# A transducer joint with its backward pass: the label rows are spread over the partitions by transfers and a VectorE shuffle, and the last chunk puts two labels on 128 partitions

## The chip, the cores and the metric

One core of one Trainium2 chip. The time is the device time of one execution in microseconds (us), the median of 3 runs for the kernel before. TensorE is PE, VectorE is DVE, ScalarE is ACT, GpSimd is POOL; SP only issues transfers.

## The reference

Inputs are bf16: `x` [2, 16000, 256], two 3-tap convolution weights `w1`, `w2`, the label rows `g` [2, 8, 256], and three 256x256 matrices. The kernel returns the output and the gradients of all seven inputs (`vjp` with `grad_out`, [2, 4000, 8, 256]).

```python
h  = gelu(conv3(x, w1))[:, ::2]           # 8000 steps
f  = gelu(conv3(h, w2))[:, ::2]           # 4000 steps
fe = f @ w_f                              # b t e
ge = g @ w_g                              # b u e, 8 rows for each b
j  = tanh(fe[:, :, None, :] + ge[:, None, :, :])
out = j @ w_o                             # b t u v
```

For each step t and each label u the forward pass needs a tanh of `fe + ge` and a 256x256 product. The gradient of `w_o` contracts `j` with `grad_out` over all t and u, with t on the partitions; the gradient with respect to `j` multiplies `grad_out` by the transpose of `w_o`.

## The kernel before

The 2 x 4000 steps are one line of 8000, cut into 17 chunks (lines 257 to 261): the first has 256 steps, 15 have 512, and the last has 64, a half block of 128. Chunk 8 holds steps of both batches, and its first 40 partitions belong to batch 0 (`c.px`, line 280). In each round of the loop at line 1069 three stages are put down for neighbouring chunks: `stage_j` for chunk k, `stage_a` (both convolutions and `fe`) for chunk k+1, `stage_de` (everything backward of `fe`) for chunk k-1.

Nothing is issued in the order of the program text. `Flow.op` records every operation with an engine (or a choice of ACT and DVE), a cost, its dependencies and a priority, the time `F.now` or `at` in units of steps. `Flow.issue` (lines 107 to 205) then simulates the engines with these costs and always takes the operation that can start first; the priority decides between operations that can start at the same time. So an operation of low priority is put wherever its engine would otherwise stand idle in the simulation. `lag` adds time to the moment from which an operation counts as ready. Each engine then runs its own operations in exactly the order found. Buffers come from classes with a fixed number of slots ("jt" 3, "gx" 3, "out" 3, "geb" 2, "ps" 7 banks of PSUM), given out in the order of the program text except for "ps".

What the change touches:

- `make_geb` (line 602) makes `GEB`, the 8 rows of `ge` of one batch on all 128 partitions. It does this by matmuls whose stationary operand is one column of `gT` repeated 128 times: 16 matmuls of 256 columns and four evacuations of 128x512 (`evac`, line 341, on ACT or DVE) for each of three versions: batch 0, batch 1, and "x", the mixture for chunk 8. The last needs `GM`, a stationary operand built by two POOL copies in an "out" buffer. `make_ge` (line 1034) makes `gT` and, separately, `GE`, the same rows with the label features on partitions.
- `stage_j`, `pair(up)`: for the labels 2up and 2up+1, ACT makes `JT` = tanh(`FE` + `GE`) with features on partitions (line 644). The gradient of `w_o` needs j with steps on partitions, `JR`. In chunks 0 and 1 (`TRANS`) PE transposes `JT` and an evacuation copies it (line 663). From chunk 2 on DVE adds `FER` and `GEB` (line 668) and ACT takes the tanh (line 673); this is the only reader of `GEB`. `FER` is `FE` transposed by PE (line 593, `rows`). Then follow the `GWO` matmuls (line 681), the products with `WOT` (line 694), a chain on DVE that sums their gradients into `NGFE` (lines 716 to 731), the output products (line 744) with evacuation into `OUT`, and one store.
- The last chunk has 64 steps and thus uses 64 of the 128 partitions in `JR`, `GO`, `OUT` and in their matmuls. `load_go` and `load_got` load `grad_out` for all eight labels at once there.
- In `stage_de`, `put` (line 940) stores the gradient of `x` from SP's queue.

```python
257    sizes = [2 * P]
258    while NP - sum(sizes) > CW:
259        sizes.append(CW)
260    sizes.append(NP - sum(sizes))
264    TRANS = (0, 1)
```

Of the kernel before, what the change touches and what calls it, by code (L numbers as in the profile page):

```python
# [12 lines left out]
ALU = mybir.AluOpType  # L13
# [207 lines left out]
def kernel(  # L221
# [99 lines left out]
    W2T = fixed([P, KT, KK * D], BF16, "W2T")  # L321
    W1T = fixed([P, KT, KK * D], BF16, "W1T")
    GR8 = fixed([U, B, D], BF16, "GR8")
    ACC1 = fixed([P, KK, KT, D], FP32, "ACC1")
# [95 lines left out]
    def load_go(k, up, at, after=()):  # L420
        c = chunks[k]
        A, Pw = c.A, c.Pw
        GO = buf("go", [P, NB, 2, V], BF16, "GO")
        if c.last:

            dma("SP", lambda: GO[:Pw].rearrange("p a u v -> p (a u v)"),
                lambda: bass.AP(tensor=go_.tensor, offset=go_.offset + c.c0 * U * V, ap=[[U * V, Pw], [1, U * V]]),
                r=[], w=[GO], bytes_=Pw * U * V * 2, new=[GO], at=at, after=after)
# [109 lines left out]
    def stage_a(k, t0, dt):  # L538
# [45 lines left out]
        for mt in range(KT):  # L584
# [13 lines left out]

    n_gwo = sum(len(c.blk) for c in chunks) * U * KT
    gwo_cnt = [0]  # L600

    def make_geb(kind):
        GEB = buf("gx" if kind == "x" else "geb", [P, U, D], BF16, "GEB")
        if kind == "x":
            px = [c.px for c in chunks if c.px is not None][0]
            GM = buf("out", [P, KT, U, P], BF16, "GM")
            for b, lo, hi in ((0, 0, px), (1, px, P)):
                op("POOL", 1200.0, lambda e, b=b, lo=lo, hi=hi: nc.gpsimd.tensor_copy(
                    out=GM[:, :, :, lo:hi], in_=gT[b][:].unsqueeze(3).to_broadcast([P, KT, U, hi - lo])),
                   r=[gT[b]], w=[(GM, b)], new=[GM] if b == 0 else [])  # L610
            rd = [GM]
        else:
            rd = [gT[kind]]
        for u2 in range(UP):
            ps = psum()

            def mms(e, u2=u2, ps=ps):
                for j in range(2):
                    u = 2 * u2 + j
                    for kt in range(KT):  # L620
                        lhsT = GM[:, kt, u, :] if kind == "x" else gT[kind][:, kt, u:u + 1].to_broadcast([P, P])
                        mm(ps[:, j * D:(j + 1) * D], lhsT, WG[:, kt, :], kt == 0, kt == KT - 1)
            op("PE", c_pe([D] * 4), mms, r=rd + [WG], w=[ps], new=[ps] + ([GEB] if u2 == 0 else []))
            evac(lambda u2=u2: GEB[:, 2 * u2:2 * u2 + 2].rearrange("p u d -> p (u d)"), lambda ps=ps: ps[:], 512,
                 r=[ps], w=[(GEB, u2)])
        return GEB

    def stage_j(k, t0, dt, GEB):
# [3 lines left out]
        FE = S["FE"]  # L632

        def pair(up):
# [4 lines left out]
            u0 = up if c.last else 0  # L639
            for j in range(2):  # L640
                for mt in range(KT):
                    def jt(e, j=j, mt=mt):
                        for b, lo, hi, _ in c.segs:
                            nc.scalar.activation(  # L644
                                out=fl(JT[:, j, mt, :W], A)[:, :, lo:hi], in_=FE[:, 0:A, mt, lo:hi], func=ACT.Tanh,
                                bias=GE[:, b, mt, 2 * up + j:2 * up + j + 1], scale=1.0)
                    op("ACT", sum(c_act((s[2] - s[1]) * A, ptr=True) for s in c.segs), jt,
                       r=[(FE, mt)] + [(GE, s[0]) for s in c.segs], w=[(JT, (j, mt))],
                       new=[JT] if j == 0 and mt == 0 else [], at=tu - q * (1.0 - (2 * j + mt) / 4), sub="jt")
            halves = [c.blk[h:h + 2] for h in range(0, A, 2)]  # L650
            for h, tbs in enumerate(halves):
                JR = buf("jr", [P, 2, 2, D], BF16, "JR")
                th = tu + q * (h / 2 - 0.5)
                n, lo, m = len(tbs), tbs[0][0], Pw
                if k in TRANS:
                    tr = psum(BF16)
# [19 lines left out]
                def gwo(e, tbs=tbs, JR=JR):  # L676
                    for tb, m in tbs:
                        for j in range(2):
# [6 lines left out]
            OUT = buf("out", [P, NB, 2, V], BF16, "OUT_SB")  # L685
            for step in range(4):
# [5 lines left out]
                def gj(e, j=j, d2=d2, ps=ps):  # L692
                    for kt in range(KT):
                        mm(fl(ps[:, :W], A), WOT[:, kt, d2 * P:(d2 + 1) * P], GOT[:, u0:u0 + A, j, kt, :Pw], kt == 0, kt == KT - 1)
                if u and d2 == 0:
                    NGZ = buf("ngz", [P, KT, CW], FP32, "NGZ")
                op("PE", c_pe([W] * KT), gj, r=[GOT, WOT], w=[ps], new=[ps, NGZ] if u and d2 == 0 else [ps])
                if d2 == 0:
                    JSQ = buf("jsq", [P, KT, CW], BF16, "JSQ")

                    def jsq(e, j=j, JSQ=JSQ):
                        if e == "ACT":
                            nc.scalar.activation(out=JSQ[:, :, :W], in_=JT[:, j, :, :W], func=ACT.Square)  # L703
                        else:
                            nc.vector.tensor_tensor(out=JSQ[:, :, :W], in0=JT[:, j, :, :W], in1=JT[:, j, :, :W], op=ALU.mult)
                    op(("ACT", "DVE"), (c_act(KT * W), c_dve(KT * W, 0.5)), jsq, r=[(JT, (j, 0)), (JT, (j, 1))], w=[JSQ],
                       new=[JSQ], at=F.now - q / 4, sub="jsq")
# [68 lines left out]
    def stage_de(k, t0, dt):  # L776
# [136 lines left out]
        for bl, m in c.sblk:  # L913
# [21 lines left out]
            if bl % 2 == 1 or bl == A - 1:  # L935
# [130 lines left out]
    make_ge()  # L1066
    GEB = make_geb(0)
    GEBX = None
    for k in range(NG + 1):
# [15 lines left out]
        if k + 1 < NG and chunks[k + 1].px is not None:  # L1085
            F.now = t0 + Wk * 0.3
            GEBX = make_geb("x")
        if k < NG:
            F.stage = "j" + part(k)
            stage_j(k, t0, Wk, GEBX if c.px is not None else GEB)  # L1090
        if k < NG and c.px is not None:
            F.now = t0 + Wk * 0.3
            GEB = make_geb(1)
        if k + 1 < NG:
# [42 lines left out]
```

## Time and profile before

| | before |
|---|---|
| median of 3 runs | 795.49 us (794.16 to 795.92) |
| the profiled execution | 793.3 us, span 791.0 us, granted PE clock 0.998 |
| busy: PE, DVE, ACT, POOL | 98%, 91%, 92%, 11% |
| HBM traffic | 51.42 MB read, 50.34 MB written |

The span runs from the first to the last record; 2.3 us of the profiled time lie around it. Busy time of PE is modelled: a matmul of 256 columns is shown with 273 ns, while in a row of such matmuls one starts every 109 ns, so a pause of less than the difference leaves no trace in the busy share. Rows of a chain or a timeline therefore show better than a share how fast PE works. "L336" is the line of the helper that issues nearly all matmuls, so groups are told apart by their tiles. "Idle before" is what an engine waited for just before an instruction, not what slowed the kernel.

### The profile page before, as it was taken

What the parts mean: (1) busy time and instruction counts of PE and PEld (TensorE: products, weight loads), DVE (VectorE), ACT (ScalarE), POOL (GpSimd) and SP (SyncE); (2) the same over time, 40 slices, a digit from 0 to 9 for tenths busy, and PEclk for the clock granted to TensorE, in tenths of its full rate; (3) what the DMA queues carried; (4) which work ended last, traced back from release to release, by engine and by line L of the source; (5) the groups of instructions that cost most, each with busy time, mean ns of one, the idle gap of its engine ahead of it and who ended that gap; (6) DMA issues with size and microseconds to landing.
All of it is one profiled execution on the core that took longest, in us unless ns stands there. A gap on an engine that the chain in (4) does not pass through costs nothing.

```text
span 791.0 us, 15682 instructions
## 1 busy us (share of the span) xinstructions
PE 773.1 (98%) x5687; PEld 537.9 (68%) x5722; DVE 716.1 (91%) x1514; ACT 727.0 (92%) x1176; POOL 83.8 (11%) x227
## 2 busy tenths in 40 slices
PE   8989999999999999999999999999999999999996
PEld 6657577576675767767677675776767767577764
DVE  5899999897998989999999898989989899899874
ACT  6999999999999998999999998999999999898752
POOL 2110010201002011110101102010020110102010
PEclk9999999999999999999999999999999999999999
DMA  9999999999999899999999999998999999999874
GB/s 208 205 190 202 214 263 229 244 228 281 202 231 256 231 238 195 229 267 219 233 218 254 228 217 233 214 264 209 230 235 214 239 237 228 237 264 255 201 177 123
DMA packets 381809, 178.82 MB, mean 226 GB/s; under 512 B 307586, under 2 KB 375460, under 8 KB 379812
## 3 DMA queue, kind: packets, MB, share of 16 engines
q1 hardware_dynamic: 380516, 177.03, 99.8%
q8 instruction: 45, 0.74, 0.4%
q10 hardware_dynamic: 1056, 0.52, 0.2%
q14 instruction: 32, 0.26, 0.1%
q0 software_dynamic: 160, 0.27, 0.1%
HBM read 51.42 MB, written 50.34 MB: 129 GB/s over the span
## 4 chain that ended last, share of the span: by engine, by line
PE 72%; ACT 11%; DVE 9%; DMA 3%; issue 3%; SPq 1%; POOL 0%; DVEq 0%; ACTq 0%
PE ps L336 60%; PE GWO L336 10%; ACT JT L644 2%; DVE g_s L516 2%; ACT JSQ L703 2%; DMA GOT<-GO 2%; ACT g_sq L510 2%; PE psb L489 2%; DVE NGZ L716 1%; ACT OUT_SB L345 1%; ACT JR L673 1%; DVE g_sq L529 1%; SPq L360 1%; ACT HTo L513 1%; DMA XC<-in_x_dram 1%
## 5 line engine op out<-in xcount | busy, mean ns | idle before, releaser
L644 ACT ACTIVATE JT<-FE,GE 128x512 bf16<-128x512 bf16 (+4 forms) x288 | 180.7, 680 | 0.0
L716 DVE SCALAR_TENSOR_TENSOR NGZ<-JSQ,ps 128x512 f32<-128x512 bf16 (+3 forms) x252 | 149.7, 607 | 2.5 <-PE ps L336 2.0
L336 PE MATMUL ps<-WO,JT 128*128 128x256 bf16 (+1 forms) x1008 | 148.2, 273 | 1.3 <-DVE NGZ L716 1.3
L336 PE MATMUL ps<-GOT,WOT 128*128 128x512 bf16 (+2 forms) x544 | 146.5, 362 | 1.8 <-DMA GOT<-GO 1.6
L345 ACT CAST OUT_SB<-ps 128x512 bf16<-128x512 f32 (+1 forms) x210 | 123.0, 600 | 17.4 <-PE ps L336 17.3
L703 ACT ACTIVATE JSQ<-JT 128x1024 bf16<-128x1024 bf16 (+2 forms) x128 | 128.6, 1005 | 9.2 <-DVE NGZ L716 8.2
L336 PEld LDWEIGHTS <-JT 128*128 128x128 bf16 (+1 forms) x1008 | 98.2, 98 | 54.9 <-issue 2.0
L336 PE MATMUL GWO<-GO,JR 128*128 128x256 bf16 (+1 forms) x1008 | 130.8, 273 | 0.1
L673 ACT ACTIVATE JR<-JR 128x1024 bf16<-128x1024 bf16 (+1 forms) x116 | 121.6, 1054 | 4.1 <-DVE JR L668 3.8
L733 DVE TENSOR_TENSOR ZS<-ZS,NGZ 128x1024 f32<-128x1024 f32 (+2 forms) x102 | 115.1, 1128 | 0.3
L336 PEld LDWEIGHTS <-JR 128*128 128x128 bf16 (+1 forms) x1008 | 98.2, 98 | 17.8 <-issue 1.3
L516 DVE SCALAR_TENSOR_TENSOR g_s<-g_sq,ps 128x512 bf16<-128x512 bf16 (+2 forms) x102 | 65.2, 639 | 41.0 <-ACT HTo L513 32.2
L336 PEld LDWEIGHTS <-W 128*128 128x128 bf16 x612 | 58.1, 98 | 59.5 <-issue 2.2
L336 PE MATMUL ps<-XC,W 128*128 128x512 bf16 (+2 forms) x408 | 84.3, 362 | 0.9 <-DMA XC<-in_x_dram 0.9
L668 DVE TENSOR_TENSOR JR<-FER,GEB 128x1024 bf16<-128x1024 bf16 (+1 forms) x116 | 79.2, 684 | 2.2 <-PE GWO L336 1.0
L336 PEld LDWEIGHTS <-X 128*128 128x128 bf16 (+1 forms) x756 | 73.8, 98 | 9.4
L772 DVE TENSOR_TENSOR ACC<-ACC,ps 128x512 f32<-128x512 f32 x90 | 59.4, 678 | 16.9 <-PE ps L336 16.7
L336 PEld LDWEIGHTS <-WOT 128*128 128x128 bf16 x544 | 51.6, 98 | 23.9 <-DMA GOT<-GO 1.8
L347 ACT ACTIVATE GX_SB<-ps 128x512 bf16<-128x512 f32 (+1 forms) x109 | 64.1, 615 | 1.6 <-PE ps L336 1.1
L510 ACT ACTIVATE g_sq<-ps 128x512 bf16<-128x512 f32 (+2 forms) x102 | 59.1, 580 | 3.4 <-PE ps L336 2.7
L525 ACT ACTIVATE g_s<-g_s 128x1024 bf16<-128x1024 bf16 (+2 forms) x51 | 52.1, 1025 | 6.3 <-DVE g_s L516 6.1
L336 PE MATMUL ps<-GHoR,X 128*128 128x256 bf16 (+1 forms) x378 | 57.7, 273 | 0.0
(139 smaller groups left out, 1113.6 us busy)
## 6 DMA issues: line engine op xcount, KB each, us to landing
GO<-in_grad_out_dram SPq DMA_DIRECT2D x60, 512.0 KB, 5.3
out_dram<-OUT_SB SPq DMA_DIRECT2D x60, 512.0 KB, 5.3
X<-in_x_dram SPq DMA_DIRECT2D x15, 1088.0 KB, 8.3
out_dram<-GX_SB SPq DMA_DIRECT2D x30, 512.0 KB, 5.5
GO<-in_grad_out_dram SPq DMA_DIRECT2D x5, 256.0 KB, 5.4
GOT<-GO SPq DMA_TRANSPOSE x65, 5.0
out_dram<-OUT_SB SPq DMA_DIRECT2D x4, 256.0 KB, 3.5
XC<-in_x_dram SPq DMA_TRANSPOSE x62, 5.5
```

Source lines behind the costliest of these rows:

```text
L336: nc.tensor.matmul(ps_ap, lhsT=lhsT, rhs=rhs, start=start, stop=stop)
L345: nc.scalar.copy(out=dst(), in_=src())
L347: nc.scalar.activation(out=dst(), in_=src(), func=ACT.Copy, scale=scale)
L510: op("ACT", c_act(W, True), lambda e, mt=mt, ps=ps: nc.scalar.activation(out=sq[:, 0:A, mt, :Pw], in_=fl(ps[:, :W], A), func=ACT.Square, s ...
L516: op("DVE", c_dve(W), lambda e, mt=mt, ps=ps: nc.vector.scalar_tensor_tensor(out=s[:, 0:A, mt, :Pw], in0=sq[:, 0:A, mt, :Pw], scalar=1.0, ...
L644: nc.scalar.activation(out=fl(JT[:, j, mt, :W], A)[:, :, lo:hi], in_=FE[:, 0:A, mt, lo:hi], func=ACT.Tanh, bias=GE[:, b, mt, 2 * up + j:2 ...
L668: op("DVE", c_dve(n * 2 * D, 0.5), lambda e, lo=lo, n=n, m=m, JR=JR: nc.vector.tensor_tensor(out=JR[:m, 0:n], in0=S["FER"][:m, lo:lo + n]. ...
L673: op("ACT", c_act(n * 2 * D), lambda e, n=n, m=m, JR=JR: nc.scalar.activation(out=JR[:m, 0:n], in_=JR[:m, 0:n], func=ACT.Tanh), r=[JR], w= ...
L703: nc.scalar.activation(out=JSQ[:, :, :W], in_=JT[:, j, :, :W], func=ACT.Square)
L716: nc.vector.scalar_tensor_tensor(out=fl(zap(), A)[:, :, lo:hi], in0=fl(JSQ[:, d2, :W], A)[:, :, lo:hi], scalar=1.0, in1=fl(ps[:, :W], A)[: ...
L733: nc.vector.tensor_tensor(out=a, in0=a, in1=b, op=ALU.add)
L772: op("DVE", c_dve(512), lambda e: nc.vector.tensor_tensor(out=acc_ap().rearrange("p k d -> p (k d)"), in0=acc_ap().rearrange("p k d -> p ( ...
```

## The change

`make_geb` no longer uses matmuls. `ge_rows` computes the 8 rows once for each batch with two matmuls and one evacuation of 8x256 into `GER`. `make_geb` clears `GEB` on POOL, copies the eight rows (4 KB) by four transfers of POOL's queue to partitions 0, 32, 64 and 96, and one `stream_shuffle` on DVE copies the first partition of each group of 32 to the other 31, with the data seen as fp32. The shuffle's `lag` is 45000 ns for batch 0 and 100000 ns for batch 1. `mix_geb` makes the mixture for chunk 8 by two DVE copies. `ge_rows` and batch 0 are put down in round k = 1, batch 1 and the mixture ahead of chunk 8.

In the last chunk the two labels of a pair lie side by side: 64 steps of one on partitions 0 to 63, of the other on 64 to 127. `GO` is loaded by two transfers, `GOT` by one transpose of 128 x 1024, `JR` comes from two PE transposes of `JT` with an evacuation of 128x256 instead of the add and the tanh (and `FER` isn't made), `GWO` and the output take two matmuls for each pair instead of four, and the output is stored by two transfers after the fourth pair instead of by one after each. The gradient of `x` for the last chunk is stored from ACT's queue.

```diff
+            for j in range(2):
+                dma("SP", lambda j=j: GO[j * Pw:(j + 1) * Pw].rearrange("p a u v -> p (a u v)")[:, 0:UP * V].rearrange(
+                        "p (a v) -> p a v", v=V),
+                    lambda j=j: bass.AP(tensor=go_.tensor, offset=go_.offset + (c.c0 * U + j) * V,
+                                        ap=[[U * V, Pw], [2 * V, UP], [1, V]]),
+                    r=[], w=[(GO, j)], bytes_=Pw * UP * V * 2, new=[GO] if j == 0 else [], at=at, after=after)
...
-            dma("SP", lambda: GOT[:, :, :, :, :Pw].rearrange("p a u k c -> p (a u k) c"),
-                lambda: GO[:Pw].rearrange("p a u v -> p (a u v)"), r=[GO], w=[GOT],
+            dma("SP", lambda: GOT[:].rearrange("p a u k c -> p (a u k) c")[:, 0:UP * KT, 0:2 * Pw],
+                lambda: GO[:2 * Pw].rearrange("p a u v -> p (a u v)")[:, 0:UP * V], r=[GO], w=[GOT],
                 bytes_=Pw * U * V * 2, new=[GOT], transpose=True, at=at)
             st[k]["GOT"] = {up: GOT for up in range(UP)}
             return
...
-        if k not in TRANS:
+        if k not in TRANS and not c.last:
             S["FER"] = rows(k, "fer", "FER", FE, 0, A, [(FE, 0), (FE, 1)], pe=Pw, lag=0.0 if c.first else 500.0)
...
-    def make_geb(kind):
-        GEB = buf("gx" if kind == "x" else "geb", [P, U, D], BF16, "GEB")
-        if kind == "x":
-            px = [c.px for c in chunks if c.px is not None][0]
-            GM = buf("out", [P, KT, U, P], BF16, "GM")
-            for b, lo, hi in ((0, 0, px), (1, px, P)):
-                op("POOL", 1200.0, lambda e, b=b, lo=lo, hi=hi: nc.gpsimd.tensor_copy(
-                    out=GM[:, :, :, lo:hi], in_=gT[b][:].unsqueeze(3).to_broadcast([P, KT, U, hi - lo])),
-                   r=[gT[b]], w=[(GM, b)], new=[GM] if b == 0 else [])
-            rd = [GM]
-        else:
-            rd = [gT[kind]]
-        for u2 in range(UP):
+    def make_geb(b):
+
+        GEB = buf("geb", [P, U, D], BF16, "GEB")
+        op("POOL", 2100.0, lambda e: nc.gpsimd.memset(GEB[:], 0.0), r=[(GER, b)], w=[GEB], new=[GEB])
+        for q in range(0, P, 32):
+            dma("POOL", lambda q=q: GEB[q:q + 1], lambda: GER[:, b, :], r=[(GER, b)], w=[(GEB, q)], bytes_=4096)
+
+        def spread(e):
+            v = GEB[:].rearrange("p u d -> p (u d)").bitcast(FP32)
+            nc.vector.stream_shuffle(v, v, [0] * 32)
+        op("DVE", 66.0 + c_dve(U * D // 2), spread, r=[GEB], w=[GEB], sub="geb", lag=45000.0 if b == 0 else 100000.0)
+        return GEB
+
+    def mix_geb(G0, G1):
+        px = [c.px for c in chunks if c.px is not None][0]
+        GEB = buf("gx", [P, U, D], BF16, "GEB")
+        op("DVE", c_dve(U * D, 0.25), lambda e: nc.vector.tensor_copy(out=GEB[:], in_=G1[:]), r=[G1], w=[GEB], new=[GEB])
+        op("DVE", c_dve(U * D, 0.25), lambda e: nc.vector.tensor_copy(out=GEB[:px], in_=G0[:px]), r=[G0], w=[GEB])
+        return GEB
...
+    def ge_rows():
+        for b in range(B):
...
+            def mms(e, b=b, ps=ps):
+                for kt in range(KT):
+                    mm(ps[:U, 0:D], gT[b][:, kt, :], WG[:, kt, :], kt == 0, kt == KT - 1)
+            op("PE", c_pe([D] * KT), mms, r=[gT[b], WG], w=[ps], new=[ps])
+            evac(lambda b=b: GER[:, b], lambda ps=ps: ps[:U, 0:D], D, r=[ps], w=[(GER, b)])
...
+                if c.last:
+                    tr = psum(BF16)
+
+                    def trs(e, tr=tr):
+                        for kt in range(KT):
+                            nc.tensor.transpose(out=tr[:2 * Pw, kt * P:(kt + 1) * P], in_=JT[:, 0, kt, :2 * Pw], identity=ident[:])
+                    op("PE", c_pe([P] * KT), trs, r=[JT, ident], w=[tr], new=[tr], at=th, sub="jr")
+                    evac(lambda JR=JR: JR[:2 * Pw, 0, 0], lambda tr=tr: tr[:2 * Pw, 0:D], D, r=[tr], w=[JR], new=[JR], f=0.58)
+                elif k in TRANS:
...
-                        for j in range(2):
+                        for j in range(1 if c.last else 2):
                             for d2 in range(KT):
                                 n = gwo_cnt[0]
-                                mm(GWO[:, d2, :], JR[:m, tb % 2, j, d2 * P:(d2 + 1) * P], GO[:m, up if c.last else tb, j, :],
+                                rhs = (GO[:2 * m].rearrange("p a u v -> p (a u v)")[:, up * V:(up + 1) * V] if c.last
+                                       else GO[:m, tb, j, :])
+                                mm(GWO[:, d2, :], JR[:2 * m if c.last else m, tb % 2, j, d2 * P:(d2 + 1) * P], rhs,
                                    n == 0, n == n_gwo - 1)
                                 gwo_cnt[0] = n + 1
-                op("PE", c_pe([V] * (4 * n)), gwo, r=[JR, GO], w=[], at=tu + q * (h / 2 + 0.3), sub="gwo")
...
+                    if c.last:
+                        def out_last(e, m=m, ps=ps):
+                            for kt in range(KT):
+                                mm(ps[:2 * m, 0:V], JT[:, 0, kt, :2 * m], WO[:, kt, :], kt == 0, kt == KT - 1)
+                        op("PE", c_pe([V] * 2), out_last, r=[JT, WO], w=[ps], new=[ps] + ([OUT] if up == 0 else []), sub="out")
+                        evac(lambda m=m: OUT[:2 * m, up, 0], lambda m=m, ps=ps: ps[:2 * m, 0:V], V, r=[ps], w=[(OUT, up)])
+                        continue
...
+            if c.last:
+                for j in range(2 if up == UP - 1 else 0):
+                    dma("SP", lambda j=j: bass.AP(tensor=o_.tensor, offset=o_.offset + (c.c0 * U + j) * V,
+                                                  ap=[[U * V, Pw], [2 * V, UP], [1, V]]),
+                        lambda j=j: OUT[j * Pw:(j + 1) * Pw, 0:UP, 0], r=[OUT], w=[], bytes_=Pw * UP * V * 2)
+                return
...
-                    dma("SP", lambda: row_ap(gx_, row + 4 * A * p0 + lo, 4 * A, p1 - p0, hi - lo),
+                    dma("ACT" if c.last else "SP", lambda: row_ap(gx_, row + 4 * A * p0 + lo, 4 * A, p1 - p0, hi - lo),
...
             F.now = t0 + Wk * 0.3
-            GEBX = make_geb("x")
+            GEB1 = make_geb(1)
+            GEBX = mix_geb(GEB, GEB1)
+        if k == 1:
+            F.now = t0 + Wk * 0.1
+            ge_rows()
+            GEB = make_geb(0)
```

Left out: the lines that name the two-label layout in the same way in the other operations of the last chunk, and the counts that follow from it.

More of the change, by code (lines that the diff above doesn't have):

```diff
@@ L597, in stage_a @@
         S["FR"] = rows(k, "fr", "FR", FT, 0, A, None, pe=Pw)
-    n_gwo = sum(len(c.blk) for c in chunks) * U * KT
+    n_gwo = sum(len(c.blk) * (UP if c.last else U) for c in chunks) * KT
     gwo_cnt = [0]
-    def make_geb(kind):
-        GEB = buf("gx" if kind == "x" else "geb", [P, U, D], BF16, "GEB")
-        if kind == "x":
-            px = [c.px for c in chunks if c.px is not None][0]
-            GM = buf("out", [P, KT, U, P], BF16, "GM")
-            for b, lo, hi in ((0, 0, px), (1, px, P)):
-                op("POOL", 1200.0, lambda e, b=b, lo=lo, hi=hi: nc.gpsimd.tensor_copy(
-                    out=GM[:, :, :, lo:hi], in_=gT[b][:].unsqueeze(3).to_broadcast([P, KT, U, hi - lo])),
-                   r=[gT[b]], w=[(GM, b)], new=[GM] if b == 0 else [])
-            rd = [GM]
-        else:
-            rd = [gT[kind]]
-        for u2 in range(UP):
-            ps = psum()
-            def mms(e, u2=u2, ps=ps):
-                for j in range(2):
[L619 to L626, printed above, removed]
@@ L632, in stage_j, with jtw @@
         FE = S["FE"]
+        def jtw(JT, j):
+            return JT[:, 0, :, j * W:(j + 1) * W] if c.last else JT[:, j, :, :W]
         def pair(up):
@@ L644, in jt @@
                             nc.scalar.activation(
-                                out=fl(JT[:, j, mt, :W], A)[:, :, lo:hi], in_=FE[:, 0:A, mt, lo:hi], func=ACT.Tanh,
+                                out=fl(jtw(JT, j)[:, mt], A)[:, :, lo:hi], in_=FE[:, 0:A, mt, lo:hi], func=ACT.Tanh,
                                 bias=GE[:, b, mt, 2 * up + j:2 * up + j + 1], scale=1.0)
@@ L677, in gwo @@
                     for tb, m in tbs:
-                        for j in range(2):
+                        for j in range(1 if c.last else 2):
                             for d2 in range(KT):
                                 n = gwo_cnt[0]
-                                mm(GWO[:, d2, :], JR[:m, tb % 2, j, d2 * P:(d2 + 1) * P], GO[:m, up if c.last else tb, j, :],
+                                rhs = (GO[:2 * m].rearrange("p a u v -> p (a u v)")[:, up * V:(up + 1) * V] if c.last
+                                       else GO[:m, tb, j, :])
+                                mm(GWO[:, d2, :], JR[:2 * m if c.last else m, tb % 2, j, d2 * P:(d2 + 1) * P], rhs,
                                    n == 0, n == n_gwo - 1)
                                 gwo_cnt[0] = n + 1
-                op("PE", c_pe([V] * (4 * n)), gwo, r=[JR, GO], w=[], at=tu + q * (h / 2 + 0.3), sub="gwo")
-            OUT = buf("out", [P, NB, 2, V], BF16, "OUT_SB")
+                op("PE", c_pe([V] * (2 if c.last else 4 * n)), gwo, r=[JR, GO], w=[], at=tu + q * (h / 2 + 0.3), sub="gwo")
+            OUT = S["OUT"] if c.last and up else buf("out", [P, NB, 2, V], BF16, "OUT_SB")
+            S["OUT"] = OUT
             for step in range(4):
@@ L693, in gj @@
                     for kt in range(KT):
-                        mm(fl(ps[:, :W], A), WOT[:, kt, d2 * P:(d2 + 1) * P], GOT[:, u0:u0 + A, j, kt, :Pw], kt == 0, kt == KT - 1)
+                        rhs = (GOT[:].rearrange("p a u k c -> p (a u k) c")[:, up * KT + kt:up * KT + kt + 1, j * Pw:(j + 1) * Pw]
+                               if c.last else GOT[:, 0:A, j, kt, :Pw])
+                        mm(fl(ps[:, :W], A), WOT[:, kt, d2 * P:(d2 + 1) * P], rhs, kt == 0, kt == KT - 1)
                 if u and d2 == 0:
@@ L702, in jsq @@
                         if e == "ACT":
-                            nc.scalar.activation(out=JSQ[:, :, :W], in_=JT[:, j, :, :W], func=ACT.Square)
+                            nc.scalar.activation(out=JSQ[:, :, :W], in_=jtw(JT, j), func=ACT.Square)
                         else:
-                            nc.vector.tensor_tensor(out=JSQ[:, :, :W], in0=JT[:, j, :, :W], in1=JT[:, j, :, :W], op=ALU.mult)
+                            nc.vector.tensor_tensor(out=JSQ[:, :, :W], in0=jtw(JT, j), in1=jtw(JT, j), op=ALU.mult)
                     op(("ACT", "DVE"), (c_act(KT * W), c_dve(KT * W, 0.5)), jsq, r=[(JT, (j, 0)), (JT, (j, 1))], w=[JSQ],
@@ L1066 @@
     make_ge()
-    GEB = make_geb(0)
-    GEBX = None
+    GEB = GEBX = None
     for k in range(NG + 1):
@@ L1091 @@
         if k < NG and c.px is not None:
-            F.now = t0 + Wk * 0.3
-            GEB = make_geb(1)
+            GEB = GEB1
         if k + 1 < NG:
```

6 lines of the change are left out of this document (1 added, 5 removed).

## The prediction

> **What bounds the kernel now.** I read the page's busy times and chain first, then windows (busy time of each engine in a stretch, with the granted clock behind them), then the rows of PE in order of time.
>
> ```profile
> PE 773.1 (98%) x5687; PEld 537.9 (68%) x5722; DVE 716.1 (91%) x1514; ACT 727.0 (92%) x1176; POOL 83.8 (11%) x227
> PE 72%; ACT 11%; DVE 9%; DMA 3%; issue 3%; SPq 1%; POOL 0%; DVEq 0%; ACTq 0%
> 25.00:45.00 20.00, 16.92 (x118) 10.21 (x117) 17.95 (x45) 19.63 (x35) 1.26 (x4) 1.00 1.16 205
> 100.00:200.00 100.00, 99.72 (x716) 68.88 (x718) 92.33 (x182) 96.24 (x149) 10.67 (x27) 1.00 1.09 248
> 763.00:777.00 14.00, 13.89 (x121) 10.89 (x121) 7.54 (x36) 6.16 (x14) 0.00 (x0) 1.00 0.75 202
> 777.00:791.00 14.00, 7.50 (x71) 4.64 (x68) 7.65 (x26) 4.01 (x10) 1.75 (x6) 0.87 0.35 96
> ```
>
> There are three stages. Until 45 us PE is not the limit: from 25 to 45 ACT is busy 19.63 of 20.00 us. From there to 777 us PE leaves nothing: 99.72 of 100, at clock 1.00. The last 14 us are a chain in which PE works half the time. Since PE's busy share is modelled, I check the middle by the period of one chunk, from the second `NGFE` product of one to that of the next:
>
> ```profile
> 282.44 0.59 PE L336 MATMUL ps<-NGFE,WFT 128*128 128x512 bf16 x2
> ...
> 330.24 0.59 PE L336 MATMUL ps<-NGFE,WFT 128*128 128x512 bf16 x2
> ...
> 379.77 0.59 PE L336 MATMUL ps<-NGFE,WFT 128*128 128x512 bf16 x2
> ...
> 427.57 0.59 PE L336 MATMUL ps<-NGFE,WFT 128*128 128x512 bf16 x2
> ```
>
> The periods are 47.80, 49.53 and 47.80 us. The middle one holds the matmuls for the mixed `GEB`:
>
> ```profile
> L336 PE MATMUL ps<-WG,GM 128*128 128x256 bf16 x16 | 2.1, 272 | 0.0
> 281.73 0.87 PE GWO L336 x8
> ```
>
> The second row gives the pace: 8 matmuls of 256 columns in 0.87 us, 0.109 each. Sixteen are 1.74 us, and 49.53 - 47.80 is 1.73. So here PE's instructions add up to the time, and one removed is its full price gained.
>
> **Mixed GEB: -1.74 us.** Those 16 matmuls go. In their place DVE gets two copies of 128x2048 bf16:
>
> ```profile
> L533 DVE TENSOR_SCALAR g_s<-g_s 128x1024 bf16<-128x1024 bf16 (+2 forms) x51 | 22.1, 433 | 0.0
> 335.33 1.21 DVE L733 TENSOR_TENSOR ZS<-ZS,NGZ 128x1024 f32<-128x1024 f32 x1
> ```
>
> By the first row, doubled, they cost at most 0.87 us each. They lie in DVE's free 7.7 of 100 us, and the four evacuations of 128x512 that leave ACT and DVE pay for them. Without that cover they are +1.7. I take 0.
>
> **The shuffles.** No shuffle is in the trace. Between the bf16 pass (0.43) and the fp32 pass over 1024 elements (1.21) I take 1.21, since the data are seen as fp32. There are two, both after 45 us under PE: 0, with +1.2 as the price where the first one delays a chain. Its reader is the first add of chunk 2:
>
> ```profile
> L668 DVE TENSOR_TENSOR JR<-FER,GEB x116: 409/682/864, 85.1 to 756.2; 128x1024 bf16<-128x1024 bf16 x112, 64x512 bf16<-64x512 bf16 x4
> ```
>
> At 85.1 us, that leaves room: rows at 15 us, POOL done by 25 (worked out below), and a lag of 45 make 70. [...]
>
> **The start: -1.3 us.** All 32 matmuls of the two plain `GEB` run here, in PE's spare time, so they themselves are worth nothing. Their evacuations are not:
>
> ```profile
> L350 DVE CAST GEB<-ps x7: 673/676/685, 14.2 to 337.7; 128x512 bf16<-128x512 f32 x7
> L345 ACT CAST GEB<-ps x5: 562/570/662, 14.8 to 345.0; 128x512 bf16<-128x512 f32 x5
> 14.94 0.47 ACT GEB L345
> ...
> 15.82 0.47 ACT GEB L345
> ...
> 28.36 0.50 ACT HTo L513
> L347 ACT ACTIVATE JR<-ps 8x256 bf16<-8x256 f32 x2 | 0.7, 373 | 0.0
> 13.30 3.22 PE L336 MATMUL ps<-WG,gT 128*128 128x256 bf16 x28
> ```
>
> The chain of waits runs through ACT from 14 to 28.9 us, two casts in it, 0.94 us. Six of DVE's seven lie in the start too (the rest of the 12 belong to the mixture). New are two evacuations of 8x256 at 0.37 or less. If only ACT's own casts count and both new ones fall on ACT, the gain is 0.2; if planning balances what is freed, it is half of 0.94 + 6 x 0.60 - 0.74, or 1.9. The row of 28 matmuls also stands ahead of the first chunk's products until 16.4. I take 1.3, nearer the upper end, because DVE's chain follows ACT's and both lose work. Ends: -1.9 and 0.
>
> **POOL in the start** is the new thing that can be late. Two clearings of 128x2048 and eight transfers come into its queue at about 15 us:
>
> ```profile
> L368 POOL MEMSET FT<- 128x512 bf16 x1 | 0.5, 520 | 0.0
> 6.86 0.75 POOL L362 DMA_DIRECT2D WG<-in_w_g_dram  x1
> 23.16 0.57 POOL L406 COPY XC<-XC 128x254 bf16<-128x254 bf16 x1 [11.30 <-DMA XC<-in_x_dram]
> 24.57 5.34 PE L336 MATMUL ps<-XC,W 128*128 128x512 bf16 x24
> 335.36 1.24 POOL L412 COPY XC<-XC_halo 128x2 bf16<-128x2 bf16 x1
> ```
>
> Clearing is four times 0.52, 2.1 us; eight transfers at 0.75 are 6.0. Together 10.2, so POOL is free at 25.2, and the three copies of `XC` that stand at 23.2 to 24.0 end at 26.0. The second half of the 24 matmuls needs them at 24.57 + 2.6 = 27.2. So this costs nothing by 1.2 us. The cover is thin, and the last row shows why: a POOL copy of 128x2 took 1.24 us, over the same stretch as the DVE operation that began at 335.33 (quoted above).
>
> [...] The trace shows one POOL operation held by one DVE operation, not more; what transfers do beside a busy DVE no row here shows.
>
> **Last chunk: -1.2 us.**
>
> ```profile
> L336 PE MATMUL GWO<-GO,JR 64*128 64x256 bf16 x16 | 2.3, 271 | 0.0
> 770.60 0.62 PE L336 MATMUL ps<-WO,JT 128*64 128x256 bf16 x4
> 53.54 0.45 PE psb L663 x8
> L673 ACT ACTIVATE JR<-JR 64x512 bf16<-64x512 bf16 x4 | 2.5, 624 | 1.2 <-DVE JR L668 1.2
> ```
>
> `GWO` goes from 16 matmuls to 8, the output (4 in each of four pairs) from 16 to 8: 16 x 0.109 = 1.74. Two transposes for `FER` go, eight for `JR` come, 0.056 each by the third row: +0.34. Net -1.40, in a stretch where PE is full. A little may come back, as these matmuls also fill waits of the backward chain of chunk 15: -1.2, ends -1.4 and 0. ACT's tanh and DVE's adds lie beside PE: 0. The two loads and the transpose carry the same bytes.
>
> **The end: -0.8 us.** Rows of SP's and ACT's queues, and SP's last wait:
>
> ```profile
> 784.97 0.98 SPq L362 DMA_DIRECT2D out_dram<-stage  x2
> 786.04 0.48 SPq L362 DMA_DIRECT2D out_dram<-GX_SB  x1
> 786.61 1.14 SPq L362 DMA_DIRECT2D out_dram<-stage  x2
> 786.70 0.42 ACTq L362 DMA_DIRECT2D out_dram<-stage  x1
> 787.80 0.40 SPq L362 DMA_DIRECT2D out_dram<-GX_SB  x1
> SPq L1132 <- DMA out_dram<-GX_SB: 1.5, 1, 1.5
> out_dram<-stage ACTq DMA_DIRECT2D x1, 128.0 KB, 2.2
> ```
>
> The program ends 1.5 us after SP's last issue at 788.2, that is at 789.7, on a `GX` store. On ACT's queue both `GX` stores can go at about 785, ahead of 786.70. The end is then ACT's own store, 786.70 + 2.2 = 788.9. Ends -1.1 (SP's queue that much shorter) and 0 (ACT's issues hold its last store up).
>
> **Sum:** -1.74 - 1.3 - 1.2 - 0.8 = -5.0. The profiled execution took 793.3 us, so 788.3; the median shown is 2.2 above it, so 790.5.
>
> **Rivals.** *Absorbed* (0.18): the start and the last chunk give nothing, since chains and not PE's sum set their ends; -1.74 - 0.8, 793.0. For it: PE is not full from 25 to 45 us nor after 777. Against it: the full window from 763 to 777 and the ACT chain's casts.
>
> *Nothing lands* (0.13): every later operation is put in a new order, and that costs what the parts give. A late period shows the size:
>
> ```profile
> 571.70 0.59 PE L336 MATMUL ps<-NGFE,WFT 128*128 128x512 bf16 x2
> ...
> 619.87 0.59 PE L336 MATMUL ps<-NGFE,WFT 128*128 128x512 bf16 x2
> ```
>
> It is 48.17, 0.37 above 47.80 for the same work; 0.3 us more in each of 15 chunks is 4.5, so 795.0. It could as well be less.
>
> *POOL late* (0.08), the slower one: each transfer is held by a DVE operation as in the row at 335.36. At the full 1.21 us each, POOL ends 9.7 later, 8.5 past the cover, and the second convolution half of chunk 1 waits: -5.0 + 8.5 gives 799.0. It decides from (1.2 + 5.0) / 8 = 0.8 us on each transfer.
>
> *Shuffle late* (0.05): the rows' evacuation has low priority; put behind the start at 45 us, with 10 us of POOL and 45 of lag, the shuffle stands at 100 instead of 70, 15 past the first add. Three `go` slots cover about one pair, 12 us; 3 us of stall, and the plan's gap again, give 796.
>
> **Numbers.** The forecast has 0.56, with its own range 788.5 to 793.5. The range 787.0 to 796.5 adds the absorbed and most of the empty case. About 0.2% (1.6 us) is what can be told from no change: faster 0.75, same 0.13, slower 0.12.
>
> **What would show it.** Right: the period with chunk 8 becomes 47.8; PE is busier than 16.92 in the window from 25 to 45 us, and doesn't wait on POOL there; the last wait is not on `GX_SB`. Wrong: a POOL row over 1.5 us near 20 us, the first `JR` add after 90, or periods above 48.3.

## The result and the profile after

| | before | changed | ratio (95% interval) |
|---|---|---|---|
| median of 9 runs each, on the same chip, us | 794.16 | 789.65 | 0.9950 (0.9933 to 0.9967) |
| profiled execution, us | 793.3 | 789.48 | |
| its span, us | 791.0 | 787.7 | |

By the ratio the change gains 4.0 us (0.5% of 794.16; the interval goes from 2.6 to 5.3); the two medians lie 4.5 apart. 790.5 was forecast, a gain of 5.0. The number came out close, but two of its terms did not: the start lost where it should have gained, and the end of the program gained almost twice what was allowed for it.

**Where the time went.** The second `NGFE` product of a chunk is the mark again. These are the first and the last such mark of the middle and the two around the mixture, in the PE rows of the changed kernel in order of time (start, duration, engine, line, operation):

```profile
140.33 0.59 PE L337 MATMUL ps<-NGFE,WFT 128*128 128x512 bf16 x2
...
331.51 0.59 PE L337 MATMUL ps<-NGFE,WFT 128*128 128x512 bf16 x2
...
379.30 0.59 PE L337 MATMUL ps<-NGFE,WFT 128*128 128x512 bf16 x2
...
716.38 0.59 PE L337 MATMUL ps<-NGFE,WFT 128*128 128x512 bf16 x2
```

The first and the last of the kernel before:

```profile
138.36 0.59 PE L336 MATMUL ps<-NGFE,WFT 128*128 128x512 bf16 x2
...
715.99 0.59 PE L336 MATMUL ps<-NGFE,WFT 128*128 128x512 bf16 x2
```

The start is 140.33 - 138.36 = 1.97 us longer. The middle is 576.05 against 577.63, 1.58 shorter, and the period with the mixture is 379.30 - 331.51 = 47.79 against 49.53. From the last mark to the end of the span it is 787.7 - 716.38 = 71.3 against 75.0, 3.7 shorter. Together that is -3.3, the difference of the spans.

**The start.** Busy times by window of the changed kernel (PE, PEld, DVE, ACT, POOL, then the granted clock):

```profile
5.00:25.00 20.00, 13.57 (x114) 10.24 (x113) 15.34 (x42) 12.58 (x32) 10.09 (x19) 0.83 1.12 209
25.00:45.00 20.00, 19.01 (x132) 11.59 (x130) 16.42 (x41) 19.05 (x34) 3.30 (x9) 1.00 0.91 191
100.00:200.00 100.00, 99.92 (x711) 68.00 (x709) 94.64 (x185) 96.44 (x150) 10.80 (x26) 1.00 1.07 241
```

The first window of the kernel before:

```profile
5.00:25.00 20.00, 17.61 (x174) 14.55 (x173) 16.82 (x56) 16.61 (x40) 3.69 (x12) 1.00 1.06 217
```

The middle is as full as it was (99.92 of 100). PE is busier from 25 to 45 us, as the prediction wanted to see (19.01 after 16.92), but only because it had fallen behind in the 20 us ahead: 13.57 after 17.61, and POOL 10.09 after 3.69. What stands there, in the changed kernel's rows in order of time (in brackets the idle time ahead of a row and what ended it):

```profile
11.88 3.54 POOL L609 MEMSET GEB<- 128x2048 bf16 x2
12.11 3.46 DVE L537 TENSOR_SCALAR g_s<-g_s 128x512 bf16<-128x512 bf16 x1
...
16.15 1.25 PE L337 MATMUL ps<-WG,gT 128*8 128x256 bf16 x4 [2.60 <-DVE g_s L520]
...
16.80 0.63 ACT L529 ACTIVATE g_s<-g_s 128x512 bf16<-128x512 bf16 x1 [3.36 <-DVE g_s L520]
```

The same DVE operation before:

```profile
12.01 0.28 DVE L533 TENSOR_SCALAR g_s<-g_s 128x512 bf16<-128x512 bf16 x1
```

An operation of 0.28 us took 3.46. It began 0.23 us after POOL's first clearing and ended with the second (15.57 against 15.42). DVE's queue stood behind it, PE waited 2.60 us and ACT 3.36 for the `g_s` that came next, and behind this wait PE's clock was granted at 0.50 from 15 to 20 us (0.83 over the whole window): the four matmuls at 16.15 took 1.25 us where such a group takes 0.60 at full clock. The clearing came at 11.88, not with the rows at 15: it writes `GEB` alone and did not wait for `GER` (written on DVE at 18.80 and 19.47); it followed POOL's operation at 11.85.

The operations on `GEB` and those that read it (number, shortest, median and longest in ns, first and last start):

```profile
L686 DVE TENSOR_TENSOR JR<-FER,GEB x112: 671/682/862, 88.2 to 735.7; 128x1024 bf16<-128x1024 bf16 x112
L363 POOL DMA_DIRECT2D GEB<-GER x8: 518/518/552, 19.8 to 25.9; - x8
L609 POOL MEMSET GEB<- x2: 1803/1803/1803, 11.9 to 13.6; 128x2048 bf16 x2
...
L615 DVE STREAM_SHUFFLE GEB<-GEB x2: 1290/1310/1331, 78.7 to 147.5; 128x1024 f32<-128x1024 f32 x2
L622 DVE COPY GEB<-GEB x1: 678/678/678, 317.5 to 317.5; 128x2048 bf16<-128x2048 bf16 x1
L623 DVE COPY GEB<-GEB x1: 674/674/674, 321.0 to 321.0; 40x2048 bf16<-40x2048 bf16 x1
```

Issuing one of these transfers took POOL 0.52 us, not 0.75, and 0.55 at most. The shuffle took 1.31 (1.21 was taken), a copy of the mixture 0.68 (0.87 at most).

**The end.** PE's rows around the last chunk's last `NGFE` product in the changed kernel:

```profile
769.34 0.34 PE L337 MATMUL ps<-GOT,WOT 128*128 128x64 bf16 x6
770.61 0.38 PE L337 MATMUL ps<-NGFE,WFT 128*128 128x64 bf16 x4 [0.93 <-DVE NGFE L753]
...
771.15 0.61 PE L337 MATMUL ps<-GHoR,X 128*128 128x256 bf16 x4
...
775.97 0.60 PE L337 MATMUL ps<-GHeR,X 128*128 128x256 bf16 x4
```

and before, where the row of the fourth output (`WO,JT` at 770.60) is in the prediction:

```profile
771.82 0.60 PE L336 MATMUL ps<-GHoR,X 128*128 128x256 bf16 x4
...
776.68 0.60 PE L336 MATMUL ps<-GHeR,X 128*128 128x256 bf16 x4
777.12 0.28 PE L336 MATMUL ps<-GOT,WOT 128*128 128x64 bf16 x4
778.48 0.38 PE L336 MATMUL ps<-NGFE,WFT 128*128 128x64 bf16 x4 [1.09 <-DVE NGFE L730]
```

The order was turned round. Before, the 48 products of chunk 15 with `X` (5.3 us) stood ahead of the last `GOT,WOT` products, so the last chunk's chain ended 7.9 us later; now the chain goes first. No line of the change says so: the planner did it. The last issues of the queues of ACT and SP, and SP's wait at the end:

```profile
781.64 2.71 SPq L363 DMA_DIRECT2D out_dram<-stage  x5
782.17 1.25 ACTq L363 DMA_DIRECT2D out_dram<-GX_SB  x2
783.87 0.41 ACTq L363 DMA_DIRECT2D out_dram<-stage  x1
```

```profile
SPq L1172 <- DMA out_dram<-GX_SB: 0.2, 1, 0.2
```

The span ends 4.9 us after PE's last matmul (782.79), before 5.4 (785.61).

### The profile page after: what moved, and what is told of

The parts are those of the page before. It is cut to its first block, busy times and chain, and to the rows that moved or that the text cites. A ratio compares the mean times of both kernels' runs of the same rounds, so it can differ in the third digit from the quotient of the medians.

```text
span 787.7 us, 15636 instructions
## 1 busy us (share of the span) xinstructions
PE 770.0 (98%) x5668; PEld 533.6 (68%) x5668; DVE 714.1 (91%) x1503; ACT 725.5 (92%) x1178; POOL 96.2 (12%) x235
## 5 line engine op out<-in xcount | busy, mean ns | idle before, releaser
L654 ACT ACTIVATE JT<-FE,GE 128x512 bf16<-128x512 bf16 (+4 forms) x288 | 185.2, 691 | 0.1
L337 PE MATMUL ps<-WO,JT 128*128 128x256 bf16 x1000 | 149.1, 273 | 0.0
L346 ACT CAST OUT_SB<-ps 128x512 bf16<-128x512 f32 (+1 forms) x215 | 129.0, 604 | 11.8 <-PE ps L337 11.7
L337 PEld LDWEIGHTS <-JT 128*128 128x128 bf16 x1000 | 97.7, 98 | 54.7 <-issue 0.2
L337 PE MATMUL GWO<-GO,JR 128*128 128x256 bf16 x1000 | 130.0, 273 | 1.5 <-ACT JR L691 0.8
L691 ACT ACTIVATE JR<-JR 128x1024 bf16<-128x1024 bf16 x112 | 120.3, 1076 | 8.4 <-DVE JR L686 8.1
L337 PEld LDWEIGHTS <-JR 128*128 128x128 bf16 x1000 | 97.5, 98 | 17.8 <-ACT JR L691 1.5
L686 DVE TENSOR_TENSOR JR<-FER,GEB 128x1024 bf16<-128x1024 bf16 x112 | 77.6, 697 | 1.5 <-PE GWO L337 1.0
L379 POOL COPY GF<-GF 128x254 bf16<-128x254 bf16 (+1 forms) x17 | 7.4, 435 | 469.4 <-issue 313.6
L337 PE MATMUL ps<-W1T,GHo 128*128 128x512 bf16 (+1 forms) x252 | 61.3, 326 | 0.0
```

The lines of the kernel that those rows point to most:

```text
L337: nc.tensor.matmul(ps_ap, lhsT=lhsT, rhs=rhs, start=start, stop=stop)
L346: nc.scalar.copy(out=dst(), in_=src())
L654: nc.scalar.activation(out=fl(jtw(JT, j)[:, mt], A)[:, :, lo:hi], in_=FE[:, 0:A, mt, lo:hi], func=ACT.Tanh, bias=GE[:, b, mt, 2 * up + j:2 ...
L686: op("DVE", c_dve(n * 2 * D, 0.5), lambda e, lo=lo, n=n, m=m, JR=JR: nc.vector.tensor_tensor(out=JR[:m, 0:n], in0=S["FER"][:m, lo:lo + n]. ...
L691: op("ACT", c_act(n * 2 * D), lambda e, n=n, m=m, JR=JR: nc.scalar.activation(out=JR[:m, 0:n], in_=JR[:m, 0:n], func=ACT.Tanh), r=[JR], w= ...
```

## The experiments

Each kernel was timed beside the kernel before. Ratios are to that; a thousandth is 0.8 us. E3 rests on 4 runs, E2 and E4 on 6, E7 on 7, the others on 10 to 12. The scatter of one profile is seen in seven kernels whose PE does the same work in the same order up to the last chunk (before, E2 and E5 to E9): their mark that stands at 138.36 above lies between 136.83 and 138.48. So a single mark is good to about 0.8 us, and what is smaller is left to the ratios.

### E1: the `GEB` part alone

```diff
 # before, with the new make_geb, mix_geb and ge_rows; the last chunk as before
-    GEB = make_geb(0)
-    GEBX = None
+    GEB = GEBX = None
...
-            GEBX = make_geb("x")
+            GEB1 = make_geb(1)
+            GEBX = mix_geb(GEB, GEB1)
+        if k == 1:
+            F.now = t0 + Wk * 0.1
+            ge_rows()
+            GEB = make_geb(0)
...
-            GEB = make_geb(1)
+            GEB = GEB1
```

> The GEB part of the change alone, the last chunk as before. Theory (the two clearings on POOL hold up one DVE operation of the first chunk, and the mixture's 16 matmuls are gained in full): a DVE TENSOR_SCALAR of over 3 us near 12 us, the start 1.3 to 2 us later than before, the period with chunk 8 at 47.8 instead of 49.5; together -0.5 to +0.5 us against the kernel before, about 794. Rival (the start is late for another reason, such as the order): no such DVE row. Rival from the prediction (the start gains 1.3): 791.

Measured: 793.73, ratio 0.9997 (0.9987 to 1.0007). Nothing is left of the mixture's 1.74. The row of DVE in order of time:

```profile
12.04 3.46 DVE L534 TENSOR_SCALAR g_s<-g_s 128x512 bf16<-128x512 bf16 x1
```

The mark of chunk 2 stands at 141.67, outside the scatter. The period with the mixture is 380.63 - 332.84 = 47.79 here too, so its gain is there. The start's loss thus belongs to this part and takes all that the part earns, about 1.5 us.

### E2: the last chunk's part alone

```diff
 # the changed kernel with make_geb as before; the last chunk and its stores as changed
-        if k == 1:
-            ge_rows()
-            GEB = make_geb(0)
+    GEB = make_geb(0)
```

> The last chunk's part alone, with its gx stores on ACT's queue; the GEB rows by matmuls as before. Theory (the last 75 us lose 3.7 us through this part alone: 1.4 of matmuls, about 0.5 at the last store, the rest waits of PE that are filled): -3.5 us, 790.5, with the start as before. Rival (1.4 and 0.8 as predicted, and the rest is the order that the GEB part brought): -2, 792. PE's wait of 1.1 us for NGFE of the last chunk tells them apart, and what follows it.

Measured: 790.71, ratio 0.9953 (0.9937 to 0.9968), -3.7 us. The changed kernel's whole gain is thus this part's, nearly twice the 2.0 that the prediction gave it (-1.2 and -0.8). PE's rows:

```profile
768.45 0.34 PE L336 MATMUL ps<-GOT,WOT 128*128 128x64 bf16 x6
769.30 0.60 PE L336 MATMUL ps<-GHoR,X 128*128 128x256 bf16 x4 [0.51 <-ACT GX_SB L347]
...
775.39 0.29 PE L336 MATMUL ps<-NGFE,WFT 128*128 128x64 bf16 x4
```

Again the `GOT,WOT` products are ahead of those with `X`, and here the last `NGFE` product stands behind both and waits for nothing.

### E3: the changed kernel with the clearings at the head of POOL's queue

```diff
+    def clear_geb():
+        for b in range(B):
+            GEB = buf("geb", [P, U, D], BF16, "GEB")
+            op("POOL", 1850.0, lambda e, GEB=GEB: nc.gpsimd.memset(GEB[:], 0.0), w=[GEB], new=[GEB], at=BIG + 1)
+            gebs.append(GEB)
...
     load_w("SP", BIG + 1)
+    clear_geb()
```

> The changed kernel with both clearings of GEB at the start of POOL's queue (2.6 to 6.3 us, when DVE has nothing to do). Theory (the clearing beside DVE is what costs the start): the DVE TENSOR_SCALAR is back at 0.28 us, PE's clock is 1.00 from 5 to 25 us, the second NGFE product of chunk 3 comes about 3 us earlier than 188.1; 786.5 us. Rival (the start is bound by ACT's order, not by the stall): within 0.5 of the changed kernel, 789.5.

Measured: 786.63, ratio 0.9901 (0.9887 to 0.9915), 7.9 us below the kernel before and about 3.9 below the changed one. It beats both. The rows of POOL and DVE in order of time:

```profile
2.63 3.57 POOL L610 MEMSET GEB<- 128x2048 bf16 x2
...
12.23 0.28 DVE L537 TENSOR_SCALAR g_s<-g_s 128x512 bf16<-128x512 bf16 x1
...
16.74 4.14 POOL L363 DMA_DIRECT2D GEB<-GER  x8 [4.67 <-DVE G L539]
```

The clearings take as long as they did, beside a DVE that has nothing to do (it waits 7.14 us, until 8.15), and the operation at 12.2 is back at 0.28. The order of the work is not what differs: up to 74 us on DVE and up to 137 us on ACT and PE, both kernels run the same operations in the same order. Two points were missed: the clock from 5 to 25 us was expected at 1.00 and is 0.91, with PE waiting for `JT` four times between 14.2 and 16.0 us (1.1 us in all), and the mark of chunk 3 comes 2.4 us earlier (185.77 for 188.13), not 3.

### E4: the kernel before with two such clearings

```diff
     make_ge()
     GEB = make_geb(0)
+    F.now = 307.0
+    for b in range(2):
+        op("POOL", 2100.0, lambda e: nc.gpsimd.memset(
+            ACC1[:].rearrange("p i k d -> p (i k d)")[:, 0:U * D // 2].bitcast(BF16), 0.0), r=[GEB], w=[ACC1])
```

> The kernel before with nothing but two clearings of 128x2048 on POOL added at the same place, into an accumulator that is written only later. Theory: the same DVE row of over 3 us and +2.5 to +3.5 us, 797. Rival (POOL's clearing alone holds nothing up): no change, 794.

Measured: 797.85, ratio 1.0052 (1.0036 to 1.0067), +4.1 us for two operations on an engine that is busy for a ninth of the span; 2.5 to 3.5 were expected. The rows of POOL, DVE and PE:

```profile
11.72 3.69 POOL L1070 MEMSET ACC<- 128x2048 bf16 x2
11.95 1.72 DVE L533 TENSOR_SCALAR g_s<-g_s 128x512 bf16<-128x512 bf16 x1
...
13.59 1.97 DVE L531 TENSOR_SCALAR g_sq<-g_sq 128x512 bf16<-128x512 bf16 x1
...
15.93 5.70 PE L336 MATMUL ps<-WG,gT 128*128 128x256 bf16 x28 [2.54 <-DVE g_s L516]
```

One held row of over 3 us was expected. Instead DVE got in between the two clearings, and each held one operation, together 3.1 us more than the usual 0.28 each. DVE and ACT run the same operations in the same order as in the kernel before, so a new order is ruled out. PE waits 2.54 us, and its 28 matmuls, 3.22 us in the kernel before, then take 5.70; from 5 to 25 us the clock is granted at 0.83, in the kernel before at 1.00. With E3 this settles the start: the clearing beside DVE is the cause, worth 4 us from either side (+4.1 put into the kernel before, -3.9 moved out of the way in the changed one).

### E5 and E6: the queue of the `GX` stores

```diff
 # E6: the kernel before with this edit; E5: E2 with this edit undone
-                    dma("SP", lambda: row_ap(gx_, ...
+                    dma("ACT" if c.last else "SP", lambda: row_ap(gx_, ...
```

> The last chunk's part alone, but with the gx stores back on SP's queue. Theory (the two stores are worth 0.5 us at the end): 0.5 us slower than with them on ACT's queue, about -3.2 against the kernel before, with the last wait on a gx store again. The prediction's size: 0.8 slower. Rival (the last transfer's own landing sets the end, wherever it is issued): no difference.

> The kernel before with nothing but the gx stores of the last chunk on ACT's queue. Theory: -0.5 us, the prediction's size -0.8, the rival 0.

Measured: E5 790.75, ratio 0.9959 (0.9946 to 0.9972), where E2 had 0.9953; E6 795.31, ratio 1.0013 (1.0000 to 1.0027). The expected gain of E6 did not come; its interval goes from no change to a loss of 2.1 us. E5 lies 0.5 us above E2, with some 1.6 to either side. So a gain from the queue was not seen, and these runs cannot size one below a us. E6's profile shows something else. The window from the last `NGFE` product to the last matmul's end, in E6:

```profile
779.18:789.40 10.22, 10.19 (x64) 5.66 (x64) 5.57 (x19) 4.22 (x10) 1.75 (x6) 0.67 0.28 79
```

and in the kernel before, whose PE has the same instructions in the same order:

```profile
778.48:785.61 7.13, 7.10 (x64) 4.38 (x64) 5.43 (x19) 4.01 (x10) 1.75 (x6) 1.00 0.24 66
```

The same 64 matmuls took 3.1 us more at a granted clock of 0.67. In the six profiles with the old order of the last chunk (before, E1, E4, E6, E8, E10) this window has the clock at 1.00 twice and at 0.66 or 0.67 four times. In the six with the new order, from the last `NGFE` product or, where the products with `X` follow it, from behind these, it has 1.00 four times (changed kernel, E2, E3, E5) and 0.79 twice (E7, E9).

### E7 and E8: the output's edit alone, and all of the last part but it

```diff
 # E7: in the last chunk one OUT for the four pairs, two labels on 128 partitions, stored after the fourth pair
-            OUT = buf("out", [P, NB, 2, V], BF16, "OUT_SB")
+            OUT = S["OUT"] if c.last and up else buf("out", [P, NB, 2, V], BF16, "OUT_SB")
+            S["OUT"] = OUT
...
+                    if c.last:
+                        def out_last(e, m=m, ps=ps):
...
 # E8: E2 with these edits undone
```

> The kernel before with nothing but the output of the last chunk from 128 rows (8 matmuls fewer, evacuations of 256 columns, one pair of stores); JR, GO and GOT as before. If matmuls alone count: -0.9 us. If this is the edit that lets the summing chain of the last chunk end ahead of chunk 15's last products: -2.5, with the products on X behind the last NGFE product.

> The last chunk's part without its output edit (GO, GOT, JR and GWO with two labels side by side, gx on ACT's queue, the output in four pieces of 64 rows as before). If matmuls and gx alone count: -0.53 - 0.5, about -1.0 us. If this part lets the summing chain end early: -2.7, with the products on X behind the last NGFE product.

Measured: E7 790.90, ratio 0.9963 (0.9949 to 0.9977), -2.9; E8 794.00, ratio 0.9995 (0.9985 to 1.0005), -0.4. So E8 cannot be told from no change (its interval goes from -1.2 to +0.4), which fits what the matmuls of `GWO` and the transposes give (8 x 0.109 - 0.34 = 0.53), and the output's edit is worth 2.9, of which its eight matmuls explain 0.87. In E7 the last `GOT,WOT` products end ahead of those with `X`, in E8 they come behind them, as before. E7's time came as expected (-2.5), its order only by half: the products with `X` were expected behind the last `NGFE` product (777.18), but start at 771.09, ahead of it.

### E9: one `OUT` buffer, and nothing else

```diff
-            OUT = buf("out", [P, NB, 2, V], BF16, "OUT_SB")
+            OUT = S["OUT"] if c.last and up else buf("out", [P, NB, 2, V], BF16, "OUT_SB")
+            S["OUT"] = OUT
+            o0 = up if c.last else 0
...
-                    evac(lambda tb=tb, m=m: OUT[:m, tb].rearrange("p u v -> p (u v)"), ...
+                    evac(lambda tb=tb + o0, m=m: OUT[:m, tb].rearrange("p u v -> p (u v)"), ...
```

> The kernel before, in which the last chunk's four pairs write their output into four places of one OUT buffer instead of taking four buffers from three slots. Every matmul, evacuation and store keeps its size, so the 16 output matmuls stay. Slot theory: the order of the last chunk changed because the fourth OUT buffer had to wait for a store; then all four outputs stand before 762 us, the last GOT,FER products stand ahead of chunk 15's products with X, as in the kernel in which only the output was edited, the last NGFE product waits for nothing, and the time falls by 1.5 to 3 us, to about 792.0 (ratio 0.996 to 0.998). Rival, the eight matmuls saved (0.87 us) and the evacuations halved made the difference: order and time as before, 794.3, ratio 0.999 to 1.001.

Measured: 791.87, ratio 0.9971 (0.9960 to 0.9982), -2.3 us with every matmul, evacuation and store of the kernel before. PE's rows:

```profile
758.58 0.62 PE L336 MATMUL ps<-WO,JT 128*64 128x256 bf16 x4
...
771.00 0.34 PE L336 MATMUL ps<-GOT,WOT 128*128 128x64 bf16 x6
771.17 0.60 PE L336 MATMUL ps<-GHoR,X 128*128 128x256 bf16 x4
...
775.98 0.60 PE L336 MATMUL ps<-GHeR,X 128*128 128x256 bf16 x4
...
777.26 0.29 PE L336 MATMUL ps<-NGFE,WFT 128*128 128x64 bf16 x4
```

The fourth output stands at 758.58, before at 770.60: there are three slots for `OUT`, and the fourth pair had to wait until a store had freed one. Without that wait the order turns round, and the last `NGFE` product waits for nothing. (The expectation's `GOT,FER` products are the `GOT,WOT` products of the rows.) From the last mark of the middle to the end of the span E9 needs 74.1 us with the last window at a granted clock of 0.79, the kernel before 75.0 at 1.00, and E6, with that kernel's order, 76.8 at 0.67.

### E10: E3 with no lag on the shuffles

```diff
-        op("DVE", 66.0 + c_dve(U * D // 2), spread, r=[GEB], w=[GEB], sub="geb", lag=45000.0 if b == 0 else 100000.0)
+        op("DVE", 66.0 + c_dve(U * D // 2), spread, r=[GEB], w=[GEB], sub="geb", lag=0.0)
```

> The changed kernel with both clearings ahead (the version that took 786.6), and with the lag of both shuffles set to 0 instead of 45 and 100 us. If the lag does what it is written for, the first shuffle is planned early, DVE stands at it until the rows have landed at about 23 us, and the start gets longer by some us: above 788, ratio above 0.992. Rival, the rows land before DVE gets there: time within 0.5 us of 786.6, ratio 0.989 to 0.991, and the shuffles stand before 60 us.

Measured: 796.54, ratio 1.0026 (1.0014 to 1.0037), 9.9 us above E3, and more than the theory of the late rows expected. DVE's rows in order of time:

```profile
26.92 1.30 DVE L620 STREAM_SHUFFLE GEB<-GEB 128x1024 f32<-128x1024 f32 x1
28.13 1.34 DVE L620 STREAM_SHUFFLE GEB<-GEB 128x1024 f32<-128x1024 f32 x1
```

DVE does not stand still ahead of them; they are 2.6 us of work in a start that has none to spare, and the mark of chunk 2 moves from 137.74 to 140.31. The larger loss comes later: from that mark to the last one E10 needs 583.2 us, E3 576.3. PE's longest waits from 100 us to the last chunk (us in all, times, longest), in E10:

```profile
PE ps L337 <- DVE g_s L520: 4.7, 7, 0.9
PE ps L337 <- ACT OUT_SB L346: 0.5, 1, 0.5
```

and in E3:

```profile
PE GWO L337 <- ACT JR L696: 0.6, 1, 0.6
PE ps L337 <- ACT FT L517: 0.3, 1, 0.3
```

Two operations moved ahead by 45 and 104 us (in E3 they start at 71.7 and 131.9) put the whole middle into another order, in which PE waits for `g_s`. These waits are 4.7 of the 6.9 us; the rest was not traced. Both theories are short of this: the lag does matter, but not because of rows that land late.

## Why the prediction was right in its number and wrong in two of its terms

- **Mixed `GEB`, -1.74: right.** 49.53 became 47.79, and the middle as a whole gained 1.58. The two copies did hide, at 0.68 each. (The 0.87 taken as their most was the doubled mean of a row with three shapes, so it was no upper bound.) The 0.16 that is missing was given back by later periods: two of them came out at 48.5 on average (427.31 to 524.22), above the limit of 48.3 that was set.
- **Shuffles, 0: right** as they were placed, at 1.31 each. E10 shows what the cover was worth: with the shuffles in the start, 9.9.
- **The start, -1.3, and POOL in it, 0: wrong; this step failed.** Together they cost about +1.5: -0.2 for E1 is the mixture's -1.74 and a loss of that size. The prediction asked when POOL would be free and who waits for POOL. It did not ask whom POOL holds. It had a row with a POOL and a DVE operation over the same stretch, and read it in one direction only, as DVE holding POOL (1.24 us for a copy whose median is 0.19). The changed kernel's trace shows the other one: beside the clearings DVE took 3.46 us for a `TENSOR_SCALAR` of 0.28. Whether DVE holds a transfer, as the rival "POOL late" had it, was hardly put to the test: the eight transfers took 0.52 to 0.55 us each, but in the stretch in which they were issued (19.8 to 26.5 us) DVE ran only casts and copies out of PSUM, products and sums: no `TENSOR_SCALAR`, and one `ZS` sum, as in the prediction's row, beside a transfer (26.03, 0.10 us after that transfer's start). That rival named the right engine and the wrong operation. Without the hold the estimate for the start stands in its sign by the times alone, of 4 and 6 runs: E3 less E2 is -4.1 us, some 1.7 to either side; with the mixture's 1.74 taken out, -2.4 is left. E3's mark (137.74) does not show that gain, so its size stays open.
- **The last chunk, -1.2, and the end, -0.8: too small, and for another reason.** E2 measured -3.7. Of the count of matmuls, what lies outside the output fits (E8: -0.4 for 0.53). The end's -0.8 was not seen (E5, E6). The rest, 2.3, is the order of the last chunk, turned by one buffer that no longer waits for a slot (E9). What the 2.3 consists of stays open. In E9 the last `NGFE` wait goes (1.1), and the granted clock behind it may give the rest: E9 is 0.9 shorter there than the kernel before at a clock of 1.00 and 2.7 shorter than E6 at 0.67. But in the two profiles at the top both clocks are 1.00, the changed kernel still waits 0.93 for `NGFE`, and it is 3.7 shorter all the same, 2.3 more than the 1.40 counted for its matmuls. How the planner gets from the slot to the order (the fourth output as the oldest user of a PSUM bank not yet issued) is argued from the code; only that the slot is the cause is shown.
- **The signs.** PE's 19.01 from 25 to 45 us was met, but as work that was late. The last wait was to leave `GX_SB` and did not: it is 0.2 us long and decides nothing. The sign against, a POOL row over 1.5 us near 20 us, was set for transfers; the row that mattered was a clearing at 11.88. The first add of `JR` came at 88.2, under the limit of 90, though the shuffle stood at 78.7 and not at 70.

The sum: -1.7 (mixture), +3.9 (hold), -2.4 (start without it), -3.7 (last chunk) is -3.9, against -4.0 measured. It closes by construction, since hold and start are both taken from E3; what stands apart from it is E4's +4.1 for the hold. The forecast of -5.0 was near by luck: a loss of 2.8 that it did not see (the start, +1.5 for -1.3) met a gain of 1.7 that it did not see either.

## What to carry to other kernels

Price an added operation on POOL not only by its own time and by who waits for it, but by what DVE does in that stretch (here 0.28 us of DVE became 3.46); a clearing that depends on nothing belongs where DVE is idle, and moving two of them was worth as much as the whole change (3.9 us and 4.0). When a planner places the work, look for a buffer class with one slot too few near the end: one wait for a store turned an order that was worth 2.3 us, more than the instructions that were counted. And test each part alone even when the total is as forecast.

## What the hardware showed that was not expected

- Two POOL clearings of 128x2048 bf16 in a row held one DVE operation through both (3.46 us in the changed kernel and in E1), or let DVE in between and held one each (1.72 and 1.97 in E4).
- After PE had waited 2.60 us at the start of the changed kernel, its clock was granted at 0.50 from 15 to 20 us; in E4, after a wait of 2.54 us, the same 28 matmuls took 5.70 us, 3.22 in the kernel before; 64 matmuls at the end took 7.13 or 10.22 us in the same order of instructions, at a granted clock of 1.00 or 0.67.
- A DVE copy of 40x2048 bf16 took as long (674 ns) as one of 128x2048 (678).
